# GpSimd's block sums and constants in another order between the spreads of means, and two query copies on VectorE

## The chip, the cores and the metric

The kernel runs on one core of one Trainium2 chip. The metric is the device time of one launch in microseconds (us), the median of several runs. The core has TensorE (PE in the profile, its weight loads PEld), VectorE (DVE), ScalarE (ACT), GpSimd (POOL) and the queue engine SyncE (SP), which here issues most of the transfers.

## The reference, cut to what matters

Three layers follow one another: an attention with a local window and one summary key and value per block of 32 positions, then two mixtures of experts. The change lies in the attention alone.

```python
def _attn_ref(q, k, v):                       # q, k, v: 2 x 8 heads x 768 x 64
    block, window = (32, 16)
    k_sum = k.reshape(B, H, nb, block, D).max(axis=3)
    v_sum = v.reshape(B, H, nb, block, D).mean(axis=3)
    scores_l = scale * np.matmul(q, k.transpose(0, 1, 3, 2))     # kept where |i - j| < 16
    scores_s = scale * np.einsum('bhsd,bhnd->bhsn', q, k_sum) + np.log(block)
    ...
    a = softmax(concatenate([scores_l_m, scores_s]))
    return np.matmul(a, np.concatenate([v, v_sum], axis=2))
# reference: attention -> _moe_ref (top 2 of 8 experts) -> _moe2_ref (top 1 of 8, skip gate)
```

## The kernel before, in words

The 16 heads are worked as 8 pairs of heads (`i` = 0 to 7), each pair in 3 groups (`g`) of 4 query blocks of 64. That makes 24 steps (`steps`, L802), and the last two pairs, 6 and 7, take turns step by step. `loop` (L878) runs 28 passes `n`, and in each pass it emits pieces of several steps in the order of the string `ORDER` (L39). Every engine executes its own instructions in exactly this order, so a piece that waits holds up all that is behind it on the same engine. `S0` is the scores of step n (`s_mm`, TensorE), `A2` the transposes of the probabilities of step n-2, `E3` their copy out on ScalarE, `N4` the normalisation of step n-4 on VectorE (`norm`), `T` transposes of keys and queries for a pair to come (`transp`, TensorE), `V3` the product with the values of step n-3 (`av_mm`), `M0` the row maxima of step n on VectorE (`s_max`), `X1` the exponentials of step n-1 on ScalarE, `P` the copies of the transposed keys and queries out of PSUM (`k_evac`, `q_evac`, `windows`), and `D` whatever the table `todo` holds for pass n.

Transposes of one key or query half go to a PSUM tile named `tp`, of which there are two. Each is emptied by two copies of 64 partitions: one for even and one for odd positions. For keys, and for the second half (`s` = 1) of queries, ScalarE makes one and VectorE the other; for the first half of queries ScalarE makes both (L447). So a pair's queries take three copies of ScalarE and one of VectorE (L445). A third transpose can't begin until the first of the two tiles is empty. For pair 6 the queries are transposed in pass 16, with the first keys of pair 7 right behind them, and for pair 7 in pass 18.

The values of a pair lie in a tile `vw`: for each query block a window of 96 rows, and under it 24 rows with the means of the value blocks. Those 24 rows are written for block 0 and then spread over the other blocks by one GpSimd copy (`spread_vs`, L330). For pairs 0 and 1 the means come from TensorE (`first_means`, `put_first`), and VectorE fills 32 of the window's rows with a copy (`next_rows`, L308). For pairs 2 to 7 GpSimd sums the blocks, two pairs to one sum (`v_sum`, n = 1 to 3): halves of 16, 8, 4, 2 and 1 positions are added (L317, L320) and scaled (L321), and `put_vs` moves the result with two small transfers that SyncE issues. The block values come by transfers whose rows are 8 KB long (32 positions of 64 numbers); in the attention nothing else comes in packets of that size. GpSimd also builds each pair's key windows (`windows`, L455 and L456) and makes constants for the routing (`numbers`, L379 to L398). VectorE uses those constants in pass 11 (`routing_constants`, L408 to L419).

The first mixture's routing of the first half of the tokens (`route1`) is interleaved from pass 17 on; the first expert's work begins on TensorE at about 111 us.

Of the kernel before, what the change touches and what calls it, by code (L numbers as in the profile page):

```python
# [18 lines left out]
B, H, S, D = 2, 8, 768, 64  # L19
BLK, WIN = 32, 16  # L20
NB = S // BLK
N, DM, E, F = 1536, 512, 8, 1024
# [12 lines left out]
A1, A2 = 4, 2  # L35
P1, P2 = 128 * A1, 128 * A2
BIG = 1.5 * 2 ** 30
SPACE = 12768
ORDER = "S0 A2 E3 N4 T V3 M0 X1 P D"  # L39
EVENTS = "m0@14 t1@16 t2@17 x0@13 m1@15 x4@15 m2@16 t0@15 x1@13 x2@14 x3@14 x5@15 x6@23 x7@24 x8@25 x9@26 x10@27 x11@27 m3@25 t3@26"  # L40
EVENTS += " A1@17 A2@18 A1@19 A1@20 A2@21 A2@22 A1@23 A1@24 A1@25 A1@26 A1@27"
EVENTS += " w0@16 w1@17 w2@18 w3@18 w4@19 w5@20 w6@21 w7@22 z0@27 z1@27 z2@27 z3@27 z4@27 z5@27 z6@27 z7@27 z8@27 z9@27 z10@27 z11@27"
# [42 lines left out]
def attention_moe(ctx, tc, q, k, v, g1, gn, noise, w1, w2, wskip, g2, w1b, w2b, out, dbg=None):  # L85
    nc = tc.nc
# [163 lines left out]
    KL, QL, VS, VW, KT, KWT, TP = {}, {}, {}, {}, {}, {}, {}  # L250
# [17 lines left out]
    VB, QB, KB = [], [], []  # L268
# [107 lines left out]
    TP = {}  # L376
# [62 lines left out]

    def q_evac(i, s):  # L440
        for u in range(2):
            dv = QB[i % 2][64 * s:64 * s + 64, :, s].rearrange("d h (m u) -> d u h m", u=2)[:, u]
            t = TP["q", s][64 * u:64 * u + 64].rearrange("d (h m) -> d h m", m=32)
            if u and s:
                tc.declare_no_dep(nc.vector.tensor_copy(dv, t).ins, one.ins, reason="they write every other column")  # L445
            else:
                one = nc.scalar.activation(dv, t, AF.Copy)  # L447

    def windows(i):
        kt = KT[i]  # L450
        kw = aa.tile([128, NH, KN], F32, name="kw", bufs=2)
        KWT[i] = kw
        ks = aa.tile([128, NB], F32, name="ks", bufs=2)
        nc.vector.tensor_reduce(ks, kt[:, WIN:WIN + S].rearrange("p (c j) -> p c j", j=BLK), AX.X, OP.max)
        nc.gpsimd.tensor_copy(kw[:, :, :KW], view(kt, 0, [[64, NH], [1, KW]]))  # L455
        (nc.gpsimd if i else nc.vector).tensor_copy(kw[:, :, KW:], ks[:, None, :].to_broadcast([128, NH, NB]))  # L456
# [344 lines left out]
    NI = B * HP  # L801
    steps = [(i, g) for i in range(NI - 2) for g in range(3)]  # L802
    steps += [(i, g) for g in range(3) for i in (NI - 2, NI - 1)]
    L = len(steps)
    todo, early, preps = {}, {}, {}

    def at(n, f, *a):
        todo.setdefault(n, []).append((f, a))
# [7 lines left out]
    def prep(i, j):  # L816
        for w, s_ in PREP[j]:
            (k_evac if w == "k" else q_evac)(i, s_)
        if j == 1:
            windows(i)  # L820

    for i in range(1, NI):
        for j in range(3):
            n = (0, 0, 1)[j] if i == 1 else 3 * i + j - (4 if i < NI - 1 else 5)
            early.setdefault(n, []).append((turn, (i, j)))
            preps.setdefault(n, []).append((prep, (i, j)))
        if i >= 2:
            at(3 * i - 3, load_v, i)
        if i >= 3:
            at(3 * i - 8, load_kq, i, "kq")  # L830
    for n in range(1, 4):
        at(6 * n - 8 if n > 1 else 0, load_vs, n)
        for k_, ws in enumerate(((16,), (8, 4), (2, 1))):
            at(6 * n - 4 + k_ if n > 1 else (3, 4, 4)[k_], v_sum, n, ws)
    for i in range(2, NI):
        at(3 * i - 1, put_vs, i)
        at(min(3 * i + 1, 21), spread_vs, i)
# [15 lines left out]
    for c in EVENTS.split():  # L853
        f, n = c.split("@")
# [10 lines left out]
    for i in range(2):  # L865
# [1 line left out]
        preps.setdefault(2 + 2 * i, []).insert(0, (put_first, (i,)))  # L867
        at(2 + 2 * i, spread_vs, i)
        at(2 + 3 * i, next_rows, i)
    at(7, numbers)  # L870
    at(5, gate_loads)
    at(11, routing_constants)

    def at_step(n, f):
        if 0 <= n < L:
            f(*steps[n])

    def loop():  # L878
        for n in range(L + 4):
            for c in ORDER.split():  # L880
                if c in "TPD":
                    for f, a in {"T": early, "P": preps, "D": todo}[c].get(n, []):
                        f(*a)
                else:
                    at_step(n - int(c[1:]), {"S": s_mm, "A": at_mm, "E": at_evac, "N": norm, "M": s_max, "V": av_mm, "X": s_exp}[c[0]])
# [132 lines left out]
    def y_out(p, a, eng=None):  # L1018
# [17 lines left out]
        if p == M2 - 1:  # L1036
            tc.declare_no_dep(SC[p, a].ins, SC["early"].ins, reason="the rows gathered early are not this expert's")

    loop()
    actx.close()  # L1040
    rp = hctx.enter_context(tc.tile_pool(name="rows", bufs=1))
# [3 lines left out]
    for c in SCRIPT.split():  # L1045
        f, a = c[0], [int(x) for x in c[1:].split(".") if x]
# [372 lines left out]
    for c in SCRIPT2.split():  # L1419
        f, a = c[0], [int(x) for x in c[1:].split(".") if x]  # L1420
# [144 lines left out]
```

## Time and profile before

| what | value |
|---|---|
| median of 3 runs | 598.69 us (595.96, 598.69, 602.15) |
| the profiled execution | 599.11 us, its span 597.3 us |
| mean granted TensorE clock | 0.982 |
| PE busy | 570.4 us, 95% |
| PEld busy | 520.4 us, 87% |
| DVE busy | 332.8 us, 56% |
| ACT busy | 251.7 us, 42% |
| POOL busy | 208.2 us, 35% |

The busy shares are averages over the whole span. The change lies in the first 100 us, so the stages there are read one by one. Times in the rows are from the start of the span.

### The profile page before, as it was taken

The numbers are of one execution on the slowest core, as the hardware profiler recorded it, in microseconds if no ns is written. First come the engines' busy times: TensorE is split into PE (matmuls) and PEld (weight loads), VectorE is DVE, ScalarE is ACT, GpSimd is POOL, SyncE is SP. The second block draws the span as 40 slices with busy tenths as digits, with TensorE's granted clock in tenths as the row PEclk, the third lists the DMA queues.
The fourth block names the chain that finished last, engine by engine and source line by source line (L and its number), as shares of the span: only waits on it lengthen the run. The fifth ranks groups of instructions, "written<-read, shape, count | busy, mean of one in ns | idle before, by whom it ended". The sixth has DMA issues, their size and how long they took to land. (4 is left out here: it accounts for less than half of the span.)

```text
span 597.3 us, 10927 instructions
## 1 busy us (share of the span) xinstructions
PE 570.4 (95%) x3971; PEld 520.4 (87%) x3971; DVE 332.8 (56%) x905; ACT 251.7 (42%) x509; POOL 208.2 (35%) x238
## 2 busy tenths in 40 slices
PE   7998987899999999999999999998989999999995
PEld 5886875699999999999999898896979988889993
DVE  5498896686563553645436464566557535610163
ACT  5497783344543334334443243344024334422341
POOL 5476723144286460712506132030343113121110
PEclk9799998999999999999999999999979999999998
DMA  9879899139575483663836547062395777689990
GB/s 206 181 142 225 230 273 305 46 103 295 150 191 162 111 213 106 135 189 105 228 124 137 183 130 170 1 158 106 90 270 170 246 270 268 220 254 268 278 313 17
DMA packets 127514, 108.54 MB, mean 182 GB/s; under 512 B 26658, under 2 KB 110706, under 8 KB 127168
## 3 DMA queue, kind: packets, MB, share of 16 engines
q1 hardware_dynamic: 117744, 86.47, 50.1%
q0 software_dynamic: 9712, 21.33, 15.2%
q8 instruction: 33, 0.54, 0.4%
q14 instruction: 25, 0.20, 0.1%
HBM read 92.49 MB, written 15.55 MB: 181 GB/s over the span
## 5 line engine op out<-in xcount | busy, mean ns | idle before, releaser
L208 DVE TENSOR_TENSOR whl<-wst,whl 128x1024 fp32r<-128x1024 f32 x88 | 107.3, 1223 | 48.3 <-ACT whl L207 45.2
L935 PE MATMUL s<-xh,whl 128*128 128x384 f32 (+6 forms) x480 | 129.7, 342 | 0.0
L958 PE MATMUL at<-hh,whl 128*128 128x280 f32 (+5 forms) x384 | 103.4, 341 | 0.0
L207 ACT ACTIVATE whl<-wst 128x1024 fp32r<-128x1024 f32 x88 | 92.1, 1052 | 0.0
L935 PEld LDWEIGHTS s<-xh,whl 128*128 128x128 f32 x480 | 87.8, 188 | 0.5
L935 PE MATMUL s<-xl,whl 128*128 128x384 f32 (+6 forms) x240 | 81.3, 339 | 0.0
L942 ACT ACTIVATE hh<-s 128x384 fp32r<-128x384 f32 (+11 forms) x80 | 35.5, 444 | 95.6 <-PE s L935 85.9
L996 PE MATMUL at<-whl,hh 128*128 128x512 f32 (+2 forms) x224 | 73.3, 402 | 0.0
L958 PEld LDWEIGHTS at<-hh,whl 128*128 128x128 f32 x384 | 69.7, 188 | 0.5
L235 POOL DMA_INDIRECT gg<-gdd,idx x29 | 32.3, 1113 | 108.2 <-DVE whole L1016 93.0
L1031 POOL DMA_INDIRECT out_dram<-whole,idx1s x29 | 49.7, 1715 | 50.9 <-DVE whole L1028 38.0
L958 PE MATMUL at<-hl,whl 128*128 128x280 f32 (+5 forms) x192 | 64.4, 335 | 0.0
L946 DVE SCALAR_TENSOR_TENSOR hl<-s,hh 128x384 fp32r<-128x384 f32 (+9 forms) x80 | 39.1, 489 | 45.3 <-ACT hh L942 37.2
L996 PEld LDWEIGHTS at<-whl,hh 128*128 128x128 f32 (+2 forms) x224 | 39.5, 177 | 11.1 <-DVE whl L208 0.2
L1357 POOL DMA_INDIRECT out_dram<-whole x14 | 14.9, 1067 | 87.8 <-DVE whole L1352 56.4
L935 PEld LDWEIGHTS s<-xl,whl 128*128 128x128 f32 x240 | 45.2, 188 | 0.2
L907 ACT ACTIVATE xh<-tp 128x512 fp32r<-128x512 f32 (+13 forms) x43 | 21.8, 515 | 48.2 <-PE tp L905 47.9
L935 PE MATMUL s<-xh,wst 128*128 128x128 f32 (+7 forms) x288 | 41.2, 289 | 0.6 <-ACT xh L907 0.6
L228 POOL DMA_INDIRECT xg<-xd,idx x29 | 32.5, 1122 | 21.3 <-DVE key L753 8.9
L909 DVE TENSOR_TENSOR xl<-tp,xh 128x512 fp32r<-128x512 f32 (+5 forms) x28 | 16.8, 610 | 41.5 <-ACT xh L907 39.3
L935 PEld LDWEIGHTS s<-xh,wst 128*128 128x128 f32 x288 | 38.0, 191 | 1.4 <-ACT xh L907 0.7
L961 ACT ACTIVATE whole<-at 128x280 f32<-128x280 f32 (+5 forms) x24 | 11.7, 488 | 60.9 <-PE at L958 58.4
(358 smaller groups left out, 979.0 us busy)
## 6 DMA issues: line engine op xcount, KB each, us to landing
wst<-in_moe_w_dram SPq DMA_DIRECT2D x128, 512.0 KB
whole<-in_k_dram SPq DMA_DIRECT2D x8, 384.0 KB
ql<-in_q_dram SPq DMA_DIRECT2D x8, 384.0 KB
xd<-whole POOLq DMA_DIRECT2D x12, 256.0 KB
out_dram<-whole SPq DMA_DIRECT2D x12, 256.0 KB
vw<-in_v_dram SPq DMA_DIRECT2D x12, 240.0 KB
vs<-in_v_dram SPq DMA_DIRECT2D x3, 768.0 KB
xg<-out_dram SPq DMA_DIRECT2D x4, 512.0 KB
```

Of the source, the lines that this page charges most:

```text
L207: nc.scalar.activation(hl[:, 0], WST[n], AF.Copy)
L208: nc.vector.tensor_tensor(hl[:, 1], WST[n], hl[:, 0].bitcast(F32), op=OP.subtract)
L228: nc.gpsimd.indirect_dma_start(out=XG[p][:r, a], out_offset=None, in_=xd[:N // 2, :] if p == 0 else xd[:, :], in_offset=bass.IndirectOffse ...
L235: nc.gpsimd.indirect_dma_start(out=GG[p][:, a], out_offset=None, in_=gdd[:N // 2, :] if p == 0 else gdd[:, :], in_offset=bass.IndirectOffs ...
L907: nc.scalar.activation(h_, t[:, :, :r], AF.Copy)
L909: nc.vector.tensor_tensor(XL[p][:, :, 128 * a:128 * a + r], t[:, :, :r], h_.bitcast(F32), op=OP.subtract)
L935: nc.tensor.matmul(t[:, :C], l_, r_, start=j == 0, stop=j == len(mm) - 1)
L942: nc.scalar.activation(hh[:, f, :C], t[:, :C], AF.Relu)
L946: nc.vector.scalar_tensor_tensor(d_[:, f, o:o + b - a], t[:, a:b], 0.0, hh[:, f, a:b].bitcast(F32), op0=OP.max, op1=OP.subtract)
L958: nc.tensor.matmul(PQ[0][:, :C], w[:, i, f], h_[:, f, :C], start=f == 0 and j == 0, stop=f == 7 and j == 2)
L996: nc.tensor.matmul(PY[p, a][:r], h_[:, f, t], w[:, i_, f % 2], start=f == 0 and j == 0, stop=f == 7 and j == len(mm) - 1, skip_group_check ...
L1031: SC[p, a] = nc.gpsimd.indirect_dma_start(out=out[:, :], out_offset=bass.IndirectOffsetOnAxis(ap=place1(idx1s, p, a)[:r], axis=0), in_=y[: ...
```

## The change

Three things are moved.

1. `v_sum`: the five sums for n = 1 go from passes 3, 4, 4 to 2, 2, 4; for n = 2 from 8, 9, 10 to 7, 8, 10; for n = 3 from 14, 15, 16 to 14, 14, 16. They are registered later, so that within a pass they now come behind `spread_vs` rather than ahead of it.
2. `numbers` goes from pass 7 to pass 4, behind the sums.
3. For pairs 6 and 7 VectorE instead of ScalarE makes the odd copy of the queries' first half. For pair 6 it stands at its place in `P`, behind the row maxima. For pair 7 both VectorE copies are put ahead of the row maxima, at a new place `F` in `ORDER`.

```diff
-ORDER = "S0 A2 E3 N4 T V3 M0 X1 P D"
+ORDER = "S0 A2 E3 N4 T V3 F M0 X1 P D"
...
     def q_evac(i, s):
         for u in range(2):
+            by_v = u and (s or i >= NI - 2)
+            if by_v and (i, s) in LASTQ:
+                continue
             dv = QB[i % 2][64 * s:64 * s + 64, :, s].rearrange("d h (m u) -> d u h m", u=2)[:, u]
             t = TP["q", s][64 * u:64 * u + 64].rearrange("d (h m) -> d h m", m=32)
-            if u and s:
+            if by_v:
                 tc.declare_no_dep(nc.vector.tensor_copy(dv, t).ins, one.ins, reason="they write every other column")
             else:
                 one = nc.scalar.activation(dv, t, AF.Copy)
+                if (i, s) in LASTQ:
+                    tc.declare_no_dep(one.ins, LASTQ[i, s].ins, reason="they write every other column")
+
+    LASTQ = {}
+
+    def q_first(i):
+
+        for s in range(2):
+            dv = QB[i % 2][64 * s:64 * s + 64, :, s].rearrange("d h (m u) -> d u h m", u=2)[:, 1]
+            LASTQ[i, s] = nc.vector.tensor_copy(dv, TP["q", s][64:128].rearrange("d (h m) -> d h m", m=32))
...
+            if i == NI - 1 and j == 2:
+                firsts[n] = [(q_first, (i,))]
...
         at(6 * n - 8 if n > 1 else 0, load_vs, n)
-        for k_, ws in enumerate(((16,), (8, 4), (2, 1))):
-            at(6 * n - 4 + k_ if n > 1 else (3, 4, 4)[k_], v_sum, n, ws)
...
         at(2 + 3 * i, next_rows, i)
-    at(7, numbers)
+
+    for n, those in ((1, (2, 2, 4)), (2, (7, 8, 10)), (3, (14, 14, 16))):
+        for m, ws in zip(those, ((16,), (8, 4), (2, 1))):
+            at(m, v_sum, n, ws)
+    at(4, numbers)
...
-                if c in "TPD":
-                    for f, a in {"T": early, "P": preps, "D": todo}[c].get(n, []):
+                if c in "TFPD":
+                    for f, a in {"T": early, "F": firsts, "P": preps, "D": todo}[c].get(n, []):
```

## Rows read from the trace of the kernel before

**Rows 1.** Busy us (instructions) by stretch: length, PE, PEld, DVE, ACT, POOL; clock, DMA share.

```profile
33.00:48.00 15.00, 14.57 (x176) 13.23 (x175) 14.05 (x64) 14.32 (x38) 11.24 (x37) 1.00 0.75 139
48.00:60.00 12.00, 9.25 (x105) 7.81 (x103) 10.72 (x48) 8.64 (x24) 6.53 (x10) 1.00 1.06 220
...
80.00:95.00 15.00, 12.40 (x162) 10.62 (x162) 14.14 (x85) 9.54 (x28) 3.36 (x3) 0.98 1.13 309
...
180.00:280.00 100.00, 100.00 (x577) 97.70 (x576) 47.53 (x64) 39.77 (x63) 40.28 (x34) 1.00 0.57 151
```

**Rows 2.** What VectorE waited for between 31.5 and 59.4 us: total, times, longest.

```profile
DVE sx L475 <- PE s L465: 0.3, 1, 0.3
```

**Rows 3.** TensorE's timeline: start, length, instructions; in brackets idle before and its releaser.

```profile
23.82 0.69 PE L501 MATMUL o<-vw,ats 120*64 120x65 f32 x16
...
35.09 0.69 PE L501 MATMUL o<-vw,ats 120*64 120x65 f32 x16 [0.43 <-DVE vw L308]
...
51.66 0.68 PE L501 MATMUL o<-vw,ats 120*64 120x65 f32 x14 [0.70 <-POOL vw L330]
...
54.84 0.52 PE L427 MATMUL tp<-ident,ql 128*128 128x128 f32 x3 [0.66 <-DVE kt L438]
...
58.16 0.63 PE L530 MATMUL tp<-ident,whole 128*128 128x128 f32 x4 [1.16 <-DVE qb L445]
...
70.92 0.55 PE L427 MATMUL tp<-ident,whole 128*128 128x128 f32 x3 [0.81 <-ACT qb L447]
...
79.84 1.12 PE L465 MATMUL s<-kw,qb 128*128 128x120 f32 x8 [1.27 <-DVE qb L445]
```

**Rows 4.** VectorE's timeline: operations whose inputs all lie in SBUF.

```profile
22.25 0.96 DVE L308 COPY vw<-vw 32x1560 f32<-32x1560 f32 x1
...
33.11 1.84 DVE L308 COPY vw<-vw 32x1560 f32<-32x1560 f32 x1
...
50.64 1.04 DVE L409 TENSOR_TENSOR wgns<-wgn,wgns 128x64 fp32r<-128x64 f32 x1
51.61 0.18 DVE L411 TENSOR_TENSOR wg2s<-wg,wg2s 128x36 fp32r<-128x36 f32 x1
...
87.88 0.82 DVE L610 TENSOR_SCALAR whole<-whole 128x12 f32<-128x12 f32 x1
```

**Rows 5.** GpSimd's timeline: spreads of means, and the key windows of pair 2.

```profile
18.50 1.36 POOL L330 COPY vw<-vw 24x1408 f32<-24x1408 f32 x1 [4.25 <-ACT vw L374]
24.92 1.15 POOL L455 COPY kw<-kt 128x1152 f32<-128x1152 f32 x1 [5.05 <-DVE kt L438]
...
32.76 1.36 POOL L330 COPY vw<-vw 24x1408 f32<-24x1408 f32 x1
...
50.24 1.36 POOL L330 COPY vw<-vw 24x1408 f32<-24x1408 f32 x1
...
87.30 1.36 POOL L330 COPY vw<-vw 24x1408 f32<-24x1408 f32 x1 [7.86 <-DMA vw<-vm]
```

**Rows 6.** GpSimd's largest block sums, grouped by shape: busy us, mean ns of one.

```profile
L317 POOL TENSOR_TENSOR vs<-vs 96x1024 f32<-96x1024 f32 x3 | 7.1, 2362 | 0.2
...
L317 POOL TENSOR_TENSOR vs<-vs 96x512 f32<-96x512 f32 x3 | 3.8, 1272 | 0.1
```

**Rows 7.** GpSimd's busy time in the stretch of the routing constants (length, busy, instructions).

```profile
40.30:42.50 2.20, 2.12 (x30) 1.00 1.19 198
```

**Rows 8.** Packets of all transfers between 18 and 19 us, by size.

```profile
DMA packets 330, 0.19 MB, mean 192 GB/s; under 512 B 16, under 2 KB 326, under 8 KB 326
```

**Rows 9.** ScalarE's copies of pair 6's queries.

```profile
69.84 1.56 ACT L447 ACTIVATE qb<-tp 64x384 f32<-64x384 f32 x3
```

**Rows 10.** VectorE's copies of the queries of pairs 6 and 7.

```profile
71.21 0.56 DVE L445 COPY qb<-tp 64x384 f32<-64x384 f32 x1
...
79.13 0.56 DVE L445 COPY qb<-tp 64x384 f32<-64x384 f32 x1
```

**Rows 11.** What VectorE waited for between 74.7 and 98 us.

```profile
DVE lg L578 <- PE s L577: 0.4, 1, 0.4
```

More of the change, by code (lines that the diff above doesn't have):

```diff
@@ L804, in attention_moe @@
     L = len(steps)
-    todo, early, preps = {}, {}, {}
+    todo, early, preps, firsts = {}, {}, {}, {}
     def at(n, f, *a):
```

## The prediction

> **What bounds the kernel now.** I began with the busy time by stretch [rows 1]. From about 112 us on TensorE is busy nearly throughout (100 of 100 us from 180 to 280), so what the attention gains or loses in its 24 steps reaches the end undiminished, and nothing the change does there can be hidden behind later work. In the attention itself TensorE has gaps: 9.25 of 12 us from 48 to 60, 12.40 of 15 from 80 to 95. VectorE is the fuller engine there, 14.05 of 15 us from 33 to 48 and 10.72 of 12 behind it. The shares alone don't tell which of the two sets the pace, so I next read what VectorE waited for: from 31.5 to 59.4 us it waited once, 0.3 us [rows 2]; from 74.7 to 98 once, 0.4 us [rows 11]. In these two stretches VectorE runs without a pause, and TensorE's waits are the echo. The third view is TensorE's timeline [rows 3]. Its waits at 35.09, 54.84, 58.16 and 79.84 name VectorE, the one at 51.66 names GpSimd's spread (0.70), the one at 70.92 ScalarE's query copies (0.81).
>
> So a wait for GpSimd that disappears is worth nothing by itself where VectorE is the pace; what VectorE saves is.
>
> **What the new order gives VectorE.** The fourth view is VectorE's own timeline, looking for one operation with two durations [rows 4]. The copy L308 took 0.96 us at 22.25 and 1.84 at 33.11, same shape. GpSimd's spread ran from 32.76 to 34.12 [rows 5]; the long copy ended at 34.95, 0.83 after the spread, nearly its whole undisturbed length. L409 took 1.04 us from 50.64 while its neighbour L411 of about half the size took 0.18; a spread ran from 50.24 to 51.60, and L409 ended at 51.68. So these VectorE operations, all of whose inputs lie in SBUF, seem to have stood still while GpSimd's copy ran. The Trainium skill has the same (SBUF — State Buffer, section "SBUF: two separate sides"): VectorE and GpSimd share one pair of ports, whoever starts first holds it for a whole instruction and the other is blocked; these rows agree.
>
> Both collisions are moved apart. First, the sums of 16, 8 and 4 leave the place ahead of the spread at 32.76. They are 2.36 and 1.27 us [rows 6] and by halving some 0.7, 4.3 in all; the constants that come in behind the spread are 2.12 us [rows 7]. GpSimd's queue, which ended at 34.12, would end at about 34.1 - 4.3 + 2.1 = 31.9, or up to 1 us later if the spread has to wait for pair 1's means. L308 at 33.11 is then alone: 1.84 - 0.96 = **0.88 us saved**, and TensorE's wait at 35.09 (0.43) goes with it. If the constants run over 33.1, the saving shrinks towards nothing. Second, the spread at 50.24 gets ahead of its sums (1.27 and by halving some 3 us with the scaling) and ends at about 48.5, so L409 at 50.64 finds GpSimd idle: 1.04 - about 0.2 = **0.83 us saved**; nothing if that spread's small transfer lands too late to let it start. TensorE's wait at 51.66 is in the same stretch and is not added: with 1.71 us taken from VectorE the waits at 54.84 and 58.16 arrive 1.7 us earlier, and TensorE, which idled 0.43 + 0.70 + 0.66 + 1.16 = 2.95 us in its listed waits [rows 3], has room for it. Next late is VectorE again, so all 1.7 us count, no more.
>
> **What the earlier sums may cost.** The first sum now stands directly behind the spread at 18.50 [rows 5]. Its values are there: between 18 and 19 us only 330 - 326 = 4 packets of block values remain [rows 8]. So it runs from about 19.9 to 22.3, then the sums of 8 and 4 to about 24.4, in a stretch where GpSimd was idle until the key windows at 24.92; those, and the queue behind them, hardly move. But L308 for pair 0 wants to run at 22.25 [rows 4], and TensorE needs its rows at 23.82 [rows 3], 0.6 us after it ended. If VectorE gets in as soon as the first sum ends, the delay is about 0.05 us and costs nothing. If GpSimd goes on with the sum of 8, L308 ends near 24.6 and TensorE waits about 0.8 us; with the sum of 4 too, 25.4 and 1.6 us. No row shows VectorE waiting beside two GpSimd operations in a row. I take nothing: L409 ended 0.08 us after the spread it had waited for, so the waiting engine is quick to begin, while GpSimd's next sum has yet to start. The Trainium skill's rule (the same section) says who holds the ports, not who is next.
>
> The sums for pairs 4 to 7 at 40 to 47 and 61 to 67 us meet VectorE operations that mostly read PSUM; I cost them at nothing, as such sums ran there before. The result for pairs 6 and 7 comes at about the same time as before, and put_vs with it. SyncE's queue carries the same transfers in the same order, some issued up to 2 us earlier; a put_vs waiting for its sum holds loads that TensorE needs only passes later, so nothing for that either.
>
> **What the query copies cost.** Pair 6: at 70.92 TensorE starts the first keys of pair 7 once ScalarE has made the second of its three copies; the three took 1.56 us from 69.84 [rows 9], so the second ended at about 70.88. That second copy becomes VectorE's, behind the row maxima, where VectorE's copy for the other half began at 71.21 and took 0.56 [rows 10]. The tile is then free at 71.77, and TensorE starts at about 71.8: **0.87 us lost**. TensorE's products with the values, the gate products and the scores of the next pass all stand behind it. ScalarE gets 0.52 us for it, with nothing to spend it on. Pair 7: the scores at 79.84 waited for VectorE's copy at 79.13, behind the row maxima [rows 3, 10]. Ahead of them, two copies would end at about 79.4, and TensorE starts 0.4 us earlier. But VectorE has no pause from there to the end of the attention [rows 11] and carries one more copy, 0.59 us with its gap; the routing's products on TensorE wait for VectorE's masks, so the 0.4 is gone some 2 us later. Of the 0.59 some 0.4 comes back: L610 at 87.88 took 0.82 us and ended at 88.70 as the spread at 87.30 ended at 88.66 [rows 4, 5]; arriving later it stands less. Left: **about 0.2 us lost**.
>
> **The sum.** -0.88 - 0.83 + 0.87 + 0.2 = -0.64 us against the profiled 599.11, which gives 598.5. That execution lies 0.42 above the median of 598.69, so the forecast for a median is 598.0: no difference that a measurement of this kernel (runs 6.2 us apart; 1%, or 6 us, is about what can be told) will show.
>
> **The rivals.**
> - Slower, by the sums in front of L308: at 22.25 the sums of 8 and 4 go ahead of the waiting copy. For it: they are queued and ready, and gaps between GpSimd's sums are short. Against: VectorE asks 0.05 us before the first sum ends. It decides from the point where L308 ends after 23.8. Price 0.8 to 1.6, at most -0.64 + 1.6 = +1.0: 599.7.
> - Faster, without the loss at 70.92: if VectorE, 1.7 us ahead after 58 us, stayed ahead of TensorE there, its copy would come before ScalarE's would have. Then -0.64 - 0.87 = -1.5: 597.2. Against: between the two places VectorE has to wait for TensorE's transposes of the first attention rows, so the lead is gone.
> - The order doesn't do what it says: the small transfers land as late as GpSimd used to be, the spreads start no earlier, and only the query copies are felt: +0.87 + 0.2 less the 0.88 at 33.11, +0.2: 598.9. Against: pair 1's spread needs no transfer at all.
>
> **How the numbers follow.** Forecast 0.5, slower rival 0.25, faster rival 0.12, the order without effect 0.1; 0.03 for something unseen. The cases span 597.2 to 599.7. The runs lie 3.5 us above and 2.7 below their median, and a median of three can lie some 2 us off; with that the range is 595.2 to 601.6. No case reaches 1% (6 us) by its mechanism, so same has 0.95; 0.02 for faster and 0.03 for slower are left to chance shifts in the tail.
>
> **What would show it.** In the changed profile L308 should have 0.96 us twice, or the first one long, which is the slower rival. L409 should take about 0.2 us, the wait at 51.66 be gone, and the passes from 58 us on begin 1.7 us earlier (or 0.1 to 0.9 with the slower rival). The wait before pair 7's first keys should name VectorE and be about 1.7 us. The scores of pair 7 should wait under 1 us. The first expert's products should start 0.6 us earlier. The forecast is wrong if the masks or spreads of the last pairs come so late that the tail from 80 to 112 us stretches by more than a microsecond, or if TensorE's clock falls in a stretch where it didn't.

## The result, and the profile after

The changed kernel took 603.82 us (median of 4 runs, 600.36 to 606.68) beside 597.33 for the kernel before (4 runs, 593.41 to 602.15): a ratio of 1.011 with a 95% interval of 1.0061 to 1.016. The forecast was 598.0 with a range of 595.2 to 601.6. Two later measurements of 12 runs each, on two other chips (f1 and g2 below), gave less: 1.0022 (0.999 to 1.0055) and 1.0029 (0.9992 to 1.0065). These and the later ratios leave out runs over 1.5% above the fastest of their kernel, which takes out some of the very executions that the change made long (one of f1's twelve, two of g2's); with all twelve the medians are 598.42 us beside 598.07, and 600.18 beside 597.30. All 32 runs of the changed kernel in this study have a median of 600.5 us, the 103 of the kernel before one of 597.5. So over the chips together it is slower, by about half a per cent, and its executions lie further apart: 13 of the 32 took 602 us or more, against 5 of 103. The 603.82 of the first four runs is therefore in part a draw of long ones.

The profiled execution took 605.53 us, its span 603.4. The timeline of TensorE in the changed kernel (start, length, instructions; in brackets the idle time before and its releaser; L478 are the scores, L514 the products with the values, and the code behind L450 has moved by 13 lines):

```profile
18.91 1.05 PE L478 MATMUL s<-kw,qb 128*128 128x120 f32 x8
...
23.13 0.69 PE L514 MATMUL o<-vw,ats 120*64 120x65 f32 x16 [2.41 <-DVE vw L308]
23.75 5.86 PE L371 MATMUL tp<-vw,sel 64*24 64x128 f32 x26
29.53 2.06 PE L478 MATMUL s<-kw,qb 128*128 128x120 f32 x8
...
36.88 1.15 PE L478 MATMUL s<-kw,qb 128*128 128x120 f32 x8
...
61.07 1.05 PE L478 MATMUL s<-kw,qb 128*128 128x120 f32 x8
...
69.91 1.05 PE L478 MATMUL s<-kw,qb 128*128 128x120 f32 x8
...
74.30 0.52 PE L427 MATMUL tp<-ident,whole 128*128 128x128 f32 x3 [1.77 <-ACT qb L450]
...
77.36 1.53 PE L478 MATMUL s<-kw,qb 128*128 128x120 f32 x8
...
84.52 1.12 PE L478 MATMUL s<-kw,qb 128*128 128x120 f32 x8 [1.06 <-DVE qb L460]
```

Two waits are new: 2.41 us for VectorE's copy L308, which [rows 3] show as no wait at 23.82, and 1.77 us before pair 7's first keys where it was 0.81. The waits at 35.09 and 51.66 are gone.

VectorE's timeline of the same execution, the operations of [rows 4] and [rows 10]:

```profile
19.98 3.01 DVE L308 COPY vw<-vw 32x1560 f32<-32x1560 f32 x1
...
37.24 0.96 DVE L308 COPY vw<-vw 32x1560 f32<-32x1560 f32 x1
...
53.89 0.21 DVE L409 TENSOR_TENSOR wgns<-wgn,wgns 128x64 fp32r<-128x64 f32 x1
...
73.64 1.15 DVE L448 COPY qb<-tp 64x384 f32<-64x384 f32 x2
...
92.47 1.07 DVE L699 SCALAR_TENSOR_TENSOR cum<-whole,na,cum 128x1 bf16<-128x1 f32 x1
```

GpSimd's timeline around pair 0's spread, with the sums of 16, 8 and 4 as one row:

```profile
17.66 1.36 POOL L330 COPY vw<-vw 24x1408 f32<-24x1408 f32 x1 [3.37 <-ACT vw L374]
19.81 5.11 POOL L317 TENSOR_TENSOR vs<-vs 96x1024 f32<-96x1024 f32 x3 [0.79 <-DMA vs<-in_v_dram]
24.86 1.14 POOL L468 COPY kw<-kt 128x1152 f32<-128x1152 f32 x1
```

Pair 1's L308 and L409 have lost their 0.88 and 0.83 us, as forecast. Pair 0's L308 has gained 2.05: it wanted to start 0.17 us behind the sum of 16 and ended at 22.99, about 0.8 us after that sum's 2.36 us [rows 6] were over. GpSimd's sums between 19 and 26 us, grouped by shape, show where it went in:

```profile
L317 POOL TENSOR_TENSOR vs<-vs 96x1024 f32<-96x1024 f32 x1 | 2.3, 2347 | 0.8 <-DMA vs<-in_v_dram 0.8
L317 POOL TENSOR_TENSOR vs<-vs 96x512 f32<-96x512 f32 x1 | 1.9, 1882 | 0.1
```

The sum of 16 has its usual length. The sum of 8 took 1.88 us instead of 1.27 [rows 6]: it stood while the copy ran, so the copy went in between the two.

The busy time by stretch (length, PE, PEld, DVE, ACT, POOL; granted clock, DMA share, GB/s) shows what followed:

```profile
16.00:20.00 4.00, 4.00 (x36) 3.54 (x34) 1.48 (x10) 1.10 (x3) 1.55 (x2) 1.00 1.01 227
20.00:24.00 4.00, 1.59 (x25) 1.26 (x24) 3.94 (x10) 3.05 (x10) 3.92 (x2) 0.97 1.29 223
24.00:34.00 10.00, 10.00 (x50) 7.76 (x50) 3.35 (x14) 1.73 (x6) 6.19 (x18) 0.50 0.64 162
...
74.00:78.00 4.00, 3.70 (x31) 3.04 (x31) 1.71 (x5) 2.12 (x6) 0.55 (x2) 0.62 0.04 8
```

Behind the wait TensorE was granted 0.50 of its clock (1.2 of 2.4 GHz) for 10 us, and again around 76 us behind the second wait. In the execution shown of the kernel before it stood at 0.57 from 16 to 24 us instead:

```profile
16.00:24.00 8.00, 8.00 (x46) 6.82 (x46) 3.15 (x17) 2.48 (x8) 1.36 (x1) 0.57 1.14 227
```

That row is the one the prediction lacked. With the clock down, TensorE's work of passes 2 and 3 came later (scores of pass 3 at 21.34 instead of 18.91). VectorE's copy of the keys that were transposed in pass 2 (L438) waited for it, and pair 0's L308 came right behind that copy, as VectorE's timeline of the kernel before shows:

```profile
21.66 0.56 DVE L438 COPY kt<-tp 64x384 f32<-64x384 f32 x1 [0.56 <-PE tp L427]
```

In an execution without that early fall it comes at about 20.0.

The start of the scores of a pass on TensorE, and of the first expert's products, in us, from the timelines of one execution each (the labels are those of the experiments):

```
execution                    pass 3  pass 6  pass 14  pass 16  pass 17  expert
before                        21.34   32.75    58.63    67.48    72.96  111.94
changed, first profile        18.91   36.88    61.07    69.91    77.36  117.90
changed, k2                   18.91   36.96    61.14    70.00    77.04  118.37
changed, k3                   19.04   36.90    61.08    69.94    76.70  118.44
changed, f1                   18.86   29.97    54.62    63.47    69.88  108.19
changed, g2                   18.54   29.65    54.68    63.53    69.94  108.45
changed, k1                   18.91   30.02    55.34    65.45    71.93  111.40
changed, k4                   21.66   32.61    57.22    67.03    73.92  115.51
g1: meeting made likelier     20.77   32.81    57.01    65.86    72.98  114.05
e1: rows first                21.32   32.73    56.91    65.76    73.33  112.03
e3: pair 6 on ScalarE         18.93   30.04    54.96    63.81    69.30  108.42
f2: queries alone             21.74   32.64    57.62    66.47    72.87  112.33
f4: rows and pair 6 first     18.96   29.64    54.15    63.00    68.60  107.02
h2: before, filled            19.07   30.18    55.17    64.03    69.51  108.31
```

### The profile page after: what moved, and what is told of

Its sections match the earlier page's. It is cut to its first block, busy times and chain, and to the rows that moved or that the text cites. A ratio compares the mean times of both kernels' runs of the same rounds, so it can differ in the third digit from the quotient of the medians.

```text
span 603.4 us, 10926 instructions
## 1 busy us (share of the span) xinstructions
PE 575.0 (95%) x3971; PEld 523.4 (87%) x3971; DVE 335.0 (56%) x907; ACT 250.4 (41%) x507; POOL 207.9 (34%) x238
```

## The experiments

Ratios are to the kernel before on the same chip, with a 95% interval.

**e1: pair 0's rows copied a pass earlier** (sums where the change put them):

```diff
-        at(2 + 3 * i, next_rows, i)
+        at(1 if i == 0 else 5, next_rows, i)
```

> The changed kernel, but VectorE's copy next_rows for pair 0 (L308) stands in pass 1 instead of pass 2, before GpSimd's first block sum starts; the sums stay where the change put them. Theory A (the sum of 16 held this copy for about 2.1 us, TensorE stood still for 2.41 us at 20.7 us, and its granted clock fell to half behind that wait): L308 takes 0.96 us, the 2.41 us wait is gone, the half-clock stretch of 24 to 33 us is gone or short, and the time is 4 to 6 us below the changed kernel's 603.8, so 598 to 600. Rival B (VectorE's two added query copies make the loss): L308 is short, but the time stays at 602 to 604. Rival C (the clock falls somewhere in the first passes in any case, as it did from 16 to 23 us in the profile before): only the wait itself is gained, 601 to 602.

Measured: 599.32 us, 1.0017 (0.9981 to 1.0053); one of its 12 runs took 2347.81 us and tells nothing of the change. VectorE's timeline of the profiled execution:

```profile
15.10 0.95 DVE L308 COPY vw<-vw 32x1560 f32<-32x1560 f32 x1
...
33.09 0.96 DVE L308 COPY vw<-vw 32x1560 f32<-32x1560 f32 x1
...
49.72 0.21 DVE L409 TENSOR_TENSOR wgns<-wgn,wgns 128x64 fp32r<-128x64 f32 x1
```

All three collisions are gone, and so is TensorE's wait. Rival B's 602 to 604 and rival C's 601 to 602 did not come. But the profiled execution had the early fall of the clock (pass 3 at 21.32), so it doesn't show the gain directly.

**e2: the first sums later**:

```diff
-    for n, those in ((1, (2, 2, 4)), (2, (7, 8, 10)), (3, (14, 14, 16))):
+    for n, those in ((1, (3, 4, 4)), (2, (7, 8, 10)), (3, (14, 14, 16))):
```

> The changed kernel with the sums for pairs 2 and 3 back in passes 3, 4, 4 (still behind the spreads of their pass). Theory A: pair 0's L308 takes 0.96 us and the wait of 2.41 us is gone, as in the run with the copy moved; the constants then end about 3 us later and may hold pair 1's L308, which gives back up to 0.9 us. 598 to 601. Rival B: 602 to 604. Rival C: 601 to 602.

Measured: 598.43 us, 1.0026 (0.9996 to 1.0056). Pair 0's L308 took 0.96 us, in an execution with the early fall (it came at 22.29). Pair 1's took 1.07 and not 1.84: it began at 33.00, while the sum of 2 ran to 33.24. The constants began only at 34.81, behind it, so this execution doesn't show what they would cost.

**e3: pair 6's query copy back on ScalarE**:

```diff
-            by_v = u and (s or i >= NI - 2)
+            by_v = u and (s or i >= NI - 1)
```

> The changed kernel with pair 6's odd query copy of the first half back on ScalarE; pair 7's stays on VectorE, ahead of the row maxima. Theory A: the wait before pair 7's first keys goes from 1.77 back to about 0.8 us, the half-clock stretch behind it (74 to 78 us) goes too, and the time falls by 1 to 2 us, to about 602; the early wait of 2.4 us stays. Rival B: 2 us or more less, near 600 or below.

Measured: 599.48 us, 1.0035 (1.0004 to 1.0066). That is rival B's time, but the 603.8 it was set against was not typical, as f1 shows. The wait before pair 7's first keys, from TensorE's timeline of this run, is as before the change, and pass 17 follows pass 16 after 5.49 us as it did before (5.48), not 7.45:

```profile
67.24 0.55 PE L427 MATMUL tp<-ident,whole 128*128 128x128 f32 x3 [0.81 <-ACT qb L450]
```

In this execution pair 0's L308 took 0.97 us although the sums stood in pass 2. That was against my expectation that the early wait stays, and it led to the race below.

**e4: the first sums' move alone, on the kernel before**:

```diff
+    for m, ws in zip((2, 2, 4), ((16,), (8, 4), (2, 1))):
+        at(m, v_sum, 1, ws)
     at(7, numbers)
```

> The kernel before with one part of the change alone: the sums for pairs 2 and 3 in passes 2, 2, 4. Theory A: pair 0's L308 takes 2 to 3 us whenever it meets the sum of 16, TensorE waits up to 2.4 us for it, and the time rises by 3 to 6 us over the kernel before. Rival B: no change, within 1 us of the kernel before. Rival C: up by 1 to 2.4 us.

Measured: 598.75 us, 1.0018 (0.9976 to 1.006), within every theory's reach by the interval. The profiled execution had the early fall, and L308 took 0.98 us at 22.30. Pair 1's took 0.96, so taking the sums from in front of its spread is enough; L409 stayed at 1.05.

**f1: the changed kernel again**, since e1, e3 and e4 came out nearer to one another than to 603.8.

> The changed kernel again, unchanged, beside the others on one chip, since its first four runs (600.4 to 606.7) may not be typical. Theory A (L308 held by the first sum, then the clock): where the clock doesn't fall in passes 1 to 3, L308 takes 3 us and the 2.4 us wait with its own fall follows; so the time is 3 to 6 us over the kernel before, 601 to 603, with few runs under 598. If those four runs were chance, it lies with the runs so far, at 598 to 600.

Measured: 598.42 us (595.82 to 606.39), 1.0022 (0.999 to 1.0055). VectorE's timeline of its profiled execution, 596.25 us:

```profile
19.93 0.96 DVE L308 COPY vw<-vw 32x1560 f32<-32x1560 f32 x1
```

GpSimd's timeline of the same execution:

```profile
20.04 5.21 POOL L317 TENSOR_TENSOR vs<-vs 96x1024 f32<-96x1024 f32 x3 [1.07 <-DMA vs<-in_v_dram]
```

The same program, and L308 starts 0.11 us ahead of the sum, which waits for its values to land; the clock didn't fall, and the first expert begins 9.7 us earlier than in the first profile. So the hold is a race between the copy and the sum, which one execution loses and another wins.

**f2: the query part alone**, on the kernel before (its sums and constants back at their passes):

```diff
-    for n, those in ((1, (2, 2, 4)), (2, (7, 8, 10)), (3, (14, 14, 16))):
-    ...
-    at(4, numbers)
+    at(7, numbers)
```

> The kernel before with the query part of the change alone (both pairs), sums and constants where they were. Theory A: the wait before pair 7's first keys is 1.7 us and names a query copy, TensorE's clock is at half for some 4 us behind it, and the step from pass 16 to 17 takes 7.5 us instead of 5.5; 1.5 to 2.5 us over the kernel before. Rival B (VectorE's load alone): the wait costs 0.9 us without a fall, and the tail behind pass 19 is 1 us longer. Rival D (the copy is worth nothing either way): within 0.5 us.

Measured: 600.14 us, 1.0018 (0.9977 to 1.0059). The wait is 1.77 us and the step from pass 16 to 17 takes 6.40 us: 0.92 more than before, without a fall of the clock behind it in this execution. The expected 7.5 us were wrong here; rival B's 0.9 fits, but its tail is longer by 0.5 us and not 1: the first expert comes 39.46 us after pass 17, before 38.98. The same wait (1.76 or 1.77 us) stands in eleven of the profiled executions. The clock fell to half behind it in seven (the first profile, k2, k3, k4, e1, e2, g1) and not in four (f1, f2, g2, k1); in the seven where the wait was under 1 us it never fell there. So the wait makes the fall possible and does not always bring it.

**f3: e1 and e3 together**, and **f4: e1 with pair 6's two copies ahead of the row maxima**, as pair 7's are:

```diff
-            if i == NI - 1 and j == 2:
+            if i >= NI - 2 and j == 2:
                 firsts[n] = [(q_first, (i,))]
```

> The changed kernel with both suspected losses undone: next_rows of pair 0 in pass 1 and pair 6's odd query copy back on ScalarE. Theory A: L308 0.96 us twice, L409 0.2, no wait of over 1 us before pair 7's first keys, pass 14 about 1.7 us earlier than before and pass 17 too; 0.5 to 2 us below the kernel before, 595.5 to 597. Rival B: pair 7's copies still load VectorE, so the time is that of the kernel before or 1 us above.

> As the run with both losses undone, but pair 6's two odd query copies stay on VectorE and go ahead of the row maxima, as pair 7's do. Theory A: the tile is free about 0.9 us earlier than in the changed kernel, the wait before pair 7's first keys is about 0.8 us without a fall of the clock; 595.5 to 597, equal to the run with the copy on ScalarE within 0.5 us. Rival B: one more copy on VectorE costs 0.6 us against that run.

Measured: f3 597.21 us, 0.9985 (0.9951 to 1.0019); f4 596.06 us, 0.9987 (0.9951 to 1.0023). Both medians lie below the kernel before and f1's 598.42 on the same chip, but neither interval leaves out no change. TensorE's timeline of f4 shows the wait at 0.96, and 5.60 us from pass 16 to 17:

```profile
66.58 0.52 PE L427 MATMUL tp<-ident,whole 128*128 128x128 f32 x3 [0.96 <-ACT qb L450]
```

**g1: the meeting made likelier**, two memsets of a tile of zeros ahead of pair 0's L308:

```diff
+        if i == 0:
+            nc.vector.memset(zero, 0.0)
+            nc.vector.memset(zero, 0.0)
         nc.vector.tensor_copy(w[64:96, :NH], w[0:32, 1:])
```

> The changed kernel with two small memsets of a tile of zeros on VectorE, about 0.3 us, ahead of pair 0's next_rows, so that L308 comes behind the start of the sum of 16 (20.0 us in a run where the clock doesn't fall before 20 us) instead of 0.1 us before or after it. Theory A: in an execution without an early fall L308 takes 3 us, TensorE waits 2 us or more and its clock falls behind that; the median is 2 to 4 us above that of the changed kernel on the same chip, and no run is below 597. If the meeting of copy and sum decides nothing: within 0.5 us of the changed kernel.

Measured: 602.64 us, all 6 runs between 601.77 and 604.81; 1.0093 (1.0059 to 1.0127). 0.34 us of VectorE's time went with 2.5 us over the changed kernel on the same chip, and left no run below 601. These times fit the theory, but the one profile does not: it had the early fall, the copy came at the sum's end (22.08) and took 1.22 us, and the execution still took 603.03 us, in the middle of the six. So such times need no hold, and g1 doesn't show what made its six runs long.

**g2: the changed kernel a third time.**

> The changed kernel a third time, on the chip of the other three of this call. Theory A, with the race at 20 us going either way: runs from 596 to 607, median 1 to 3 us over the kernel before, 599 to 601.

Measured: 600.18 us (595.0 to 606.89), 1.0029 (0.9992 to 1.0065). In the profiled execution (596.95 us) L308 came at 19.61, the sum at 19.99.

**h1 and h2: a matmul in TensorE's early wait**, on f4 and on the kernel before:

```diff
+    at(1, keep_busy, 1)
     for i in range(2):
         at(1 + 2 * i, first_means, i)
```

> The changed kernel with next_rows of pair 0 in pass 1 and pair 6's query copies ahead of the row maxima, and one more matmul of the identity (128x512, its result unused) on TensorE in pass 1, where it waits 0.8 us at 13.3 us. Theory: the early fall of the clock (16 to 23 us in five of ten profiles) comes from that wait; filled, no execution has it, scores of pass 3 begin at about 19.1 us, and the median falls by 1 to 2 us against the same kernel without it, to 594.5 to 595.5. If the fall has another cause: 596, as without.

> The kernel before with that one matmul in pass 1 alone. Theory: scores of pass 3 at 19.1 us instead of 21.3, median 1 to 2 us below the kernel before. If the fall has another cause: within 0.5 us of it.

Measured: h1 597.10 us, 1.0006 (0.9978 to 1.0034); h2 598.09 us, 1.0011 (0.9985 to 1.0038). Neither profile has the early fall (pass 3 at 18.84 and 19.07), but the medians fell by nothing. So filling that wait is no gain, and what starts the early fall stays open: one profile each doesn't tell, since the fall is missing from profiles without the filler too (h1's 597.10 was taken on another chip than f4's 596.06).

**k1 to k4: four more executions of the changed kernel.**

> One more execution of the changed kernel with its profile. Theory A: either L308 of pair 0 takes 2.5 us or more, the granted clock falls behind it, and the execution takes 602 us or more; or it takes about 1 us and the execution takes 595 to 601. The other theory (the slow executions come from falls of the clock elsewhere): the time doesn't go with L308's length.

> Second of four looks at the changed kernel. Theory A: L308 of pair 0 of 2.5 us or more goes with 602 us or more, about 1 us with 595 to 601. The other theory: the time doesn't go with L308.

> Third of four looks at the changed kernel. Theory A: L308 of pair 0 of 2.5 us or more goes with 602 us or more, about 1 us with 595 to 601. The other theory: the time doesn't go with L308.

> Fourth of four looks at the changed kernel. Theory A: L308 of pair 0 of 2.5 us or more goes with 602 us or more, about 1 us with 595 to 601. The other theory: the time doesn't go with L308.

Measured, with the three earlier profiles of the same program:

```
execution      L308 start, length   sum of 16 starts   clock low behind it   us
first profile  19.98  3.01          19.81              24 to 34              605.53
k2             19.98  3.13          19.94              24 to 35              603.75
k3             20.11  2.95          19.88              25 to 35              607.34
k1             19.98  0.97          20.01              no                    599.91
f1             19.93  0.96          20.04              no                    596.25
g2             19.61  0.96          19.99              no                    596.95
k4             22.57  0.96          20.26              low from 15 to 22     603.90
```

GpSimd's timeline of k1 at that place, the sum 0.03 us behind L308's start at 19.98:

```profile
20.01 5.29 POOL L317 TENSOR_TENSOR vs<-vs 96x1024 f32<-96x1024 f32 x3 [0.98 <-DMA vs<-in_v_dram]
```

And GpSimd's timeline of k2, the sum 0.04 us ahead of it:

```profile
19.94 5.11 POOL L317 TENSOR_TENSOR vs<-vs 96x1024 f32<-96x1024 f32 x3 [0.91 <-DMA vs<-in_v_dram]
```

The sum in k1 is not free of the meeting either: of its 5.29 us the sum of 16 alone took 3.16 instead of 2.35, so here it stood for the copy.

In six of seven the time goes with L308's length. k4 takes 603.90 us without a hold: its clock was low at 15, 57, 74 and 98 us. So the other theory has a part too, and the granted clock shows how large. From the granted clock in slices of 0.5 us I summed how long TensorE was at half before the first expert's work (a slice between the two levels counted by its share):

```
execution      hold   at half, us   first expert   us
f1             no      0.0          108.19         596.25
g2             no      0.0          108.45         596.95
k1             no      6.8          111.40         599.91
g1             no     17.1          114.05         603.03
k4             no     20.5          115.51         603.90
first profile  yes    20.5          117.90         605.53
k2             yes    20.5          118.37         603.75
k3             yes    20.5          118.44         607.34
```

The first expert comes the later, the longer the clock was at half. With as much time at half, the executions with the hold are another 2.4 to 2.9 us behind k4, about the length of the wait. So the hold is one of several ways to a long time: it costs its wait, and the fall behind it, and k4 reached the same time at half by falls elsewhere.

Counting runs of 602 us or more says the same. With pair 0's rows a pass earlier (e1, f3, f4, h1) there is none in 47 runs, beside the 2347.81 us; the changed kernel has 13 in 32. But e2 and f2, where the sum of 16 does not stand in front of pair 0's copy, have three in twelve each, with 609.39 us in f2, and no profile shows one of those.

## Why the prediction was wrong, point by point

**What failed: the paragraph on what the earlier sums may cost.** The step is "L308 for pair 0 wants to run at 22.25": I took that time from one execution and built a margin of 0.05 us on it, without looking at the granted clock there, which stood at half from 16 to 23 us. Without that fall L308 comes at 19.6 to 20.1, at the start of the sum of 16 and not at its end. That GpSimd could start "at about 19.9" came out right (19.81 to 20.04), but by luck: I added the spread's length to a start from the same slowed execution. Without the fall the spread ends at 18.7 to 19.2, and the sum waits for its transfer. The packets of 8 KB had passed by 19 us, as I read them (none from 19 to 20 in these executions); yet the profile names the transfer as what released the sum, at 19.81 at the earliest, and that delay I left out. So copy and sum are level, and the transfer decides. Where the sum is first the copy stands for all of it. The sum of the prediction put this term at nothing; it measured 2.41 us of TensorE's wait and a half clock behind it.

The slower rival named the place and the mechanism, but its road was not taken: GpSimd never went on with the sums of 8 and 4 ahead of the waiting copy. The waiting engine came next, as I had assumed, and the price was still larger than the rival's 1.6 us. The Trainium skill (SBUF — State Buffer, section "SBUF: two separate sides") says that the one who starts first holds the shared ports for a whole instruction; the six executions without an early fall agree, on both sides of the race, down to 0.03 us. The prediction's own signs of being wrong came too: the clock fell in stretches where it had not (24 to 34 and 74 to 78 us), and the tail from pass 17 to the first expert grew by 1.6 us.

**The price.** With the hold, scores of pass 6 start at 36.9 us; without it and without an early fall at 29.65 to 30.02. That is 6.9 us, of which the wait itself is 2.3 to 2.5; the rest goes with the half clock from 24 to 34 us, where the 26 small matmuls of L371 took 5.86 us (3.13 in their undisturbed turn at 14.09). That the fall comes from the wait is argued from order and not shown by an experiment: it follows all three holds and none of the three executions without hold or early fall. Against the execution shown of before, which had lost 2.4 us to its early fall, the hold cost 4.1 us by pass 6.

**The gain** of 1.71 us was right for the pair of executions compared: from pass 6 to 14 the kernel before took 25.88 us, the first profile, k2, k3 and e1 24.18 or 24.19. But it isn't what the kernel gains as a rule. With the old sums and constants f2 and h2 took 24.98 and 24.99 us, since pair 1's L308 was not held there (0.96 us); the spread stood for it instead, 2.10 and 2.09 us. So the 0.88 rested on one draw as well, and 0.8 us are left against f2. Where the early passes are quick even those go: f1 took 24.65 us, g2 25.03 and k1 25.32, h2 24.99. There the transfers are next. TensorE waited 0.92, 1.25 and 1.10 us at 45.5 us for a pair's keys to land, which it did not in h2, and pair 3's spread waited for its means (1.79 us in f1) and met L409 again (0.30, 0.64 and 0.64 us against 0.21).

**Pair 6's copy** was priced at 0.87 us. From pass 16 to 17 it measured 0.92 and 0.93 in f2 and f1, right; but in the first profile 1.97, in e1 2.09, with the clock at half behind the wait. The sum had no term for such a fall. The row of that wait names ScalarE, whose copies had ended 1.0 us before it did: the second wait, for VectorE's copy (73.64 and half of 1.15, so 74.2), is the one that ended last.

**Pair 7's copies** gave half of what was forecast: its scores waited 1.06 us instead of 1.27, 0.21 less and not 0.4, and the masks of the routing took the gain back, 0.35 us on TensorE. L610 (L623 in the changed kernel) was relieved, 0.17 us, but L699 stood in its place (1.07 us against 0.22), beside the last spread from 92.16 to 93.52, so the 0.4 on VectorE did not come back.

**Summed up for the first profile**: +4.1 at pass 6, -1.7 to pass 14, nothing to 16, +2.0 to 17, and +1.6 from there to the first expert (38.98 us before, 40.54 after), where the clock was at half for about 7 us and not 3.5: +6.0, of the 6.4 between the two executions' times. What brought the longer fall in the tail stays open. The forecast had +0, -1.7, +0.9 and +0.2. For executions in which the copy wins and no early fall comes, "no difference" holds: f1 and g2 reach the first expert at 108.2 and 108.5, h2 with the old order at 108.3. The 0.6 us of gain they don't show, all the less as h2's clock fell from 93 to 96 us and theirs not at all.

## What to carry to other kernels

Before a margin of a tenth of a microsecond is read from a profile, look at the granted clock in front of it, and at a second execution: here one clock fall had moved the copy by 2.3 us. When work is put into GpSimd's idle time, list every VectorE operation with all its inputs in SBUF that can run beside it, at its earliest time too, and not only at the time shown; and if one of them stands on TensorE's path, move it out of reach, as f4 does with a pass. A kernel whose times spread over 10 us needs more than four runs to tell a per cent: four gave 1.011 here, twelve 1.0022 and 1.0029.

## What the runs showed of the hardware

- A VectorE copy waiting for a GpSimd operation goes in between two GpSimd operations that are queued back to back: L308 ended about 0.8 us after the sum of 16 in three executions, and the sum of 8 behind it took 1.88 us instead of 1.27.
- A few hundredths of a microsecond decide: the sum 0.03 us behind the copy (k1) cost TensorE nothing, and stood itself, 3.16 us instead of 2.35; 0.04 ahead of it (k2) it cost 2.2 us on VectorE, and the scores of pass 6 came 6.9 us later.
- The same program ran from 595.0 to 607.34 us, with TensorE's mean granted clock from 0.994 to 0.972, and where in the attention it fell differed from execution to execution. All five runs above 606 us had 0.972, all six below 597 us 0.986 or more.
- The same wait of 1.77 us on TensorE was followed by half the clock in some executions and not in others.
